# Attention, gated product and squared-ReLU layers on one core: the order of ScalarE and VectorE in attention written out by hand, and the first w3·w_out products in float32

## The chip, the cores and the metric

The kernel runs on one core of a Trainium2 chip. The metric is the device time of one execution in microseconds (us). The program before has a median of 604.52 us over 3 runs (602.40 to 607.51); the one execution that the profiler recorded took 602.16 us, of which 600.4 us lie between the first and the last instruction (the span).

## The reference, cut to what matters

```
attn:   scores = q kᵀ / 8, causal mask, softmax over keys (sum + 1e-9), times v
        2 batches x 12 heads x 448 tokens x 64
moe:    h = ((x w1) * (x w2)) w3 ;  y = h w_out        768 -> 1024 -> 1024 -> 768
moe2:   r = max(y w_in, 0) ; out = (r * r) w_out2      768 -> 2048 -> 768
```

There are 896 tokens. The weights come as float64 (8 bytes), all the rest as float32.

## The kernel before, in words

The matrix W = w3·w_out does not depend on the tokens, so it is worked out once, on TensorE, in between the steps of attention; then h·w_out needs one product by W in place of two. W has 16 rows of w3 blocks (two groups g of 8, `w3` 0 to 15) by 2 column halves: 32 *units*, each made by `w_half` from one w3 block and four w_out blocks, in one PSUM bank (`acc`), which is then copied or added into `wraw`.

A product of two float32 matrices is made of three matmuls of type fp32r: each factor is split into a high part and the rest (hi·hi + hi·lo + lo·hi). A unit is thus 4 blocks x 3 = 12 matmuls of 128x128 by 384 columns. A weight block goes through these steps before it can be used:

- `load`: one DMA into a raw buffer (3 of them, `RAW`), on the SP queue,
- `to_f32`: float64 to float32, by a Prelu on ScalarE (ACT), a tensor_scalar on the low words on VectorE (DVE) and a shift-and-or (scalar_tensor_tensor) on DVE,
- `two_parts`: a cast to fp32r on ACT (the high part) and a subtraction on DVE (the low part).

Attention goes over 12 pairs of heads in 13 *slots*. In slot p TensorE (PE) has: the scores of pair p (`s`), a unit, the transposes of the probabilities of pair p-1 (`pp`, 20 of them, copied out of PSUM to `pt` by ACT), a unit, the product with v of pair p-1 (`x`), a unit. `fill` says where units are made: after each of three gaps of a slot, from gap `LEAD` on. For each head the softmax has four blocks of rows; each takes a fused minimum on DVE (custom instruction, from PSUM, into `p`), an exponential with a row sum on ACT, and, after two small operations on `st` on DVE, a division by the sum (tensor_scalar on `p`) on GpSimd (POOL), or on DVE for pair 0. The `x` product is split into two fp32r parts in `xT` by ACT and DVE.

PSUM has 2 banks (`ps_w`) that `acc` of the units and `x` share in turn, and 6 banks (`ps_a`) that the score tiles (6 for a pair) and the `pp` tiles (6 for a pair) share in turn. So a unit waits until what was in its bank two turns ago has been copied out, and transposes wait until the minima have read the scores.

The order of PE's instructions in attention is as the code writes it (`manual_schedule` with PE). On DVE, ACT, POOL and the SP queue a scheduler at build time sets the order, from priorities (`high_priority`, `AHEAD`, `FAR_AHEAD`, `issue_after`) and its own estimate of time. On the chip every engine runs its instructions strictly in that order; an instruction that waits holds up all behind it.

After attention TensorE goes through x·w1, x·w2, h = ab·W, g = h·w_in and g·w_out2, with weights converted in the same way into a ring of 8 buffers.

Of the kernel before, what the change touches and what calls it, by code (L numbers as in the profile page):

```python
# [17 lines left out]
def attention_moe_moe2(ctx: ExitStack, tc: tile.TileContext, qk, v, w1, w2, w3, w_out, w_in2, w_out2, out):  # L18
# [11 lines left out]

    nc = tc.nc
    NP_ALL, P, S2 = qk.shape
    S = S2 // 2
# [14 lines left out]
    RING = 8  # L48
    RAW = 3
    LEAD = 7  # L50
    EARLY = 2
    AHEAD, FAR_AHEAD = 120, 400

# [20 lines left out]
    def to_f32(key):  # L74
        t = raws.pop(key)
        n = t.shape[1]
        low, high = t[:, :, 0], t[:, :, 1]
        x = rawp.tile([P, DM], F32, tag="x", name=f"x_{key[0]}_{key[1]}", bufs=2)[:, :n]
        nc.scalar.activation(x, high.bitcast(F32), AF.Prelu, scale=2.0 ** -112, alpha=-2.0 ** 32)  # L79
        nc.vector.tensor_scalar(low, low, 2.0 ** -29, 7.0, ALU.mult, ALU.min)  # L80
        nc.vector.scalar_tensor_tensor(  # L81
            x.bitcast(U32), x.bitcast(U32), 3, low, op0=ALU.logical_shift_left, op1=ALU.bitwise_or)
        f32s[key] = x
# [16 lines left out]
    for g in range(N3 // KF):  # L100
        for i in range(KF):
            order += [("w3", g * KF + i)]
            if g == 0 and i == 0:
                order += [("wout", f) for f in range(NB)]
            if g == 0 and i % 2 == 1:
                order += [("wout", NB + i // 2)]
# [13 lines left out]
    def make_f32(n):  # L120
        for key in order[made["f32"]:n]:
            make_loads(made["f32"] + 1)
            if key[0] != "W":
                to_f32(key)
            made["f32"] += 1

    def make(key):

        while made["hl"] <= place[key]:
            i = made["hl"]  # L130
            nm, n = at = order[i]
            make_f32(i + 2)
            make_loads(i + 2 + RAW)
            if nm == "w3":
                t = w3p[0].tile([P, 2, W3N], F32R, tag="w3", name=f"w3_{n}", bufs=2)
            else:
                t = ringp.tile([P, 2, DM], F32R, tag="ring", name=f"hl_{nm}_{n}")
            two_parts(t[:, 0], t[:, 1], wraw[:, n, :] if nm == "W" else f32s.pop(at))
            hls[at] = t
# [11 lines left out]
    with (  # L151
# [14 lines left out]
        st_t, p_t, pt_t = {}, {}, {}  # L166
# [14 lines left out]
        def scores(p):  # L181

# [12 lines left out]
            for g in BLOCKS:  # L195
                for i in g:
                    w = (i + 1) * CP
                    for j in range(2):
                        own = slice(j * D, (j + 1) * D)
                        mm(ps[j, i], y[own, 0, i * CP:w], y[own, 1, :w], True, True)  # L200
            for j in range(2):
                for g in BLOCKS:
                    for i in g:
                        last["min"] = nc.vector.tensor_tensor_reduce(  # L204
                            p_t[2 * p + j][:, off[i]:off[i + 1]], ps[j, i], mask[:, S - (i + 1) * CP:], QS, 3.0e38,
                            ALU.add, ALU.min, st_t[p][:, 0, j, i:i + 1],
                        ).ins

        def softmax(p, j):

            st = st_t[p][:, :, j]
            blocks = [(i, p_t[2 * p + j][:, off[i]:off[i + 1]]) for g in BLOCKS for i in g]
            for i, e in blocks:
                nc.scalar.activation(e, e, AF.Exp, bias=st[:, 0, i:i + 1], scale=-1.0,  # L214
                                     accum_out=st[:, 1, i:i + 1])
            nc.vector.tensor_scalar(st[:, 2], st[:, 1], 1.0e-9, None, ALU.add)
            nc.vector.reciprocal(st[:, 3], st[:, 2])
            engine = nc.vector if p < 1 else nc.gpsimd
            for i, e in blocks:
                engine.tensor_scalar(e, e, st[:, 3, i:i + 1], None, ALU.mult)  # L220
# [3 lines left out]
        def p_transposes(h):  # L224
            pt = p_t.pop(h)
            t = att.tile([CP, off[NCH]], F32, tag="pt", name=f"pt{h}", bufs=3)
            for gi, g in enumerate(((0,), (1,), (2, 3))):
# [8 lines left out]
                last["pt"] = nc.scalar.copy(t[:, coff[g[0]]:coff[g[0]] + o], x[:CP, :o]).ins  # L236
            pt_t[h] = t

        def attend(p):
# [3 lines left out]
            for c in range(NCH):  # L243
                for j in range(2):
# [3 lines left out]
                       c == 0, c == NCH - 1)  # L248
            b, kk = p // NPAIR, p % NPAIR
            hi, lo = (xT[:, s, kk, b * S:(b + 1) * S] for s in range(2))  # L250
            two_parts(hi, lo, x)
# [3 lines left out]
        last = {}  # L255

        def w_half(g, i, n):
# [3 lines left out]
            for f in range(NB):  # L261
                with tc.high_priority(AHEAD):
                    make(("wout", g * NB + f))
                    make(("w3", min(n3 + 1, N3 - 1)))
                t, c = hls["w3", n3], slice(f * P, (f + 1) * P)
                wo = hls["wout", g * NB + f]
# [227 lines left out]
```

## Time and profile before

| | |
|---|---|
| median of 3 runs | 604.52 us (602.40 to 607.51) |
| profiled execution | 602.16 us, span 600.4 us |
| PE busy | 573.8 us (96%) |
| DVE busy | 282.8 us (47%) |
| ACT busy | 275.3 us (46%) |
| POOL busy | 163.9 us (27%) |
| mean granted TensorE clock | 0.98 |

Attention and the units end at 184.7 us; from there on TensorE alone works through the dense layers. The page cuts the span in 40 slices of 15 us: PE's first slices are the ones below nine tenths, and in the second and third the granted clock (tenths of full speed) is 6 and 7. Busy shares are averages over stages that have different limits, so they are read stage by stage. A duration of one instruction includes its latency; instructions that follow each other at once overlap by some tens of ns, so that a start-to-start distance is a little shorter.

### The profile page before, as it was taken

The page shows a single profiled execution, that of the slowest core. Times are in us where ns is not written, and L with a number is a line of the kernel's source. Part 1 is how long each engine was busy: PE and PEld are TensorE (multiplying, and loading weights), DVE is VectorE, ACT ScalarE, POOL GpSimd, SP SyncE. Part 2 cuts the span into 40 slices and gives each one's busy share as a digit, 9 for nine tenths or more (in the row PEclk, how much of TensorE's full clock was granted, in tenths as well). Part 3 has the DMA queues.
Part 4 walks back from the last instruction along what each step waited for, and adds up shares of the span by engine and source line. Part 5 has one row for each costly group of instructions (what it writes and reads, how often), then busy time and mean ns, then how long its engine had stood idle before and what let it go on. Part 6 is the DMA issues. An engine that isn't in the chain of part 4 may idle for free.

```text
span 600.4 us, 8072 instructions
## 1 busy us (share of the span) xinstructions
PE 573.8 (96%) x3120; PEld 511.3 (85%) x3120; DVE 282.8 (47%) x557; ACT 275.3 (46%) x584; POOL 163.9 (27%) x144
## 2 busy tenths in 40 slices
PE   5769898999989999999999999999999999999997
PEld 3458676888779999999999999999999999999997
DVE  4877576676766555411120177555300875421111
ACT  5877776676765433222210166555301755551000
POOL 1285677557650211111110001333100013331000
PEclk9679999999989999999999999999999999999999
DMA  8664334432345343300000056333300663000111
GB/s 300 239 217 150 133 117 153 123 106 91 130 160 219 139 159 105 106 1 1 0 1 1 0 198 222 106 105 106 106 0 1 208 224 118 29 2 27 52 53 52
DMA packets 14821, 63.95 MB, mean 107 GB/s; under 512 B 1664, under 2 KB 1920, under 8 KB 14784
## 3 DMA queue, kind: packets, MB, share of 16 engines
q1 hardware_dynamic: 14784, 63.45, 31.2%
q8 instruction: 24, 0.39, 0.3%
q14 instruction: 13, 0.11, 0.1%
HBM read 60.69 MB, written 2.75 MB: 106 GB/s over the span
## 4 chain that ended last, share of the span: by engine, by line
PE 78%; DVE 8%; DMA 7%; ACT 4%; issue 1%; SPq 0%; DVEq 0%
PE w L63 25%; PE g L63 20%; PE o L63 19%; PE h L63 10%; DMA raw_w<-in_w 7%; DVE p L204 2%; PE x L63 2%; PE pp L232 2%; DVE x_w L81 1%; ACT p L214 1%; ACT pt L236 1%; PE s L63 1%; DVE raw_w L80 1%; DVE x_wout L81 1%; DMA raw_wout<-in_w_out 1%
## 5 line engine op out<-in xcount | busy, mean ns | idle before, releaser
L220 POOL TENSOR_SCALAR p<-p,st 112x448 f32<-112x448 f32 (+1 forms) x88 | 99.9, 1152 | 72.9 <-ACT p L214 24.7
L63 PE MATMUL w<-xT,hl_w 128*128 128x448 f32 x576 | 119.5, 368 | 0.0
L63 PE MATMUL g<-hT,hl_win 128*128 128x448 f32 x576 | 119.4, 368 | 0.0
L63 PEld LDWEIGHTS w<-xT,hl_w 128*128 128x128 f32 x576 | 108.0, 188 | 11.0
L63 PEld LDWEIGHTS g<-hT,hl_win 128*128 128x128 f32 x576 | 108.1, 188 | 10.9
L63 PE MATMUL o<-hl_wout,gT 128*128 128x384 f32 x672 | 116.8, 334 | 0.0
L63 PEld LDWEIGHTS o<-hl_wout,gT 128*128 128x128 f32 x672 | 116.5, 188 | 0.1
L87 POOL TENSOR_TENSOR gT<-r,gT 128x448 fp32r<-128x448 f32 x32 | 40.1, 1275 | 198.1 <-ACT gT L86 130.1
L63 PE MATMUL w<-hl_wout,w 128*128 128x384 f32 x384 | 77.6, 351 | 5.0 <-ACT wraw L275 2.6
L63 PEld LDWEIGHTS w<-hl_wout,w 128*128 128x128 f32 x384 | 67.8, 194 | 9.6 <-ACT wraw L275 3.0
L214 ACT ACTIVATE p<-p,st 112x112 f32<-112x112 f32 (+2 forms) x96 | 50.2, 536 | 21.4 <-DVE st L204 21.4
L63 PE MATMUL h<-abT,hl_W 128*128 128x448 f32 x288 | 59.7, 368 | 0.0
L63 PEld LDWEIGHTS h<-abT,hl_W 128*128 128x128 f32 x288 | 54.1, 188 | 5.5
L87 POOL TENSOR_TENSOR abT<-a,abT 128x448 fp32r<-128x448 f32 x16 | 22.3, 1408 | 108.4 <-ACT abT L86 108.4
L87 DVE TENSOR_TENSOR hl_wout<-x_wout,hl_wout 128x768 fp32r<-128x768 f32 x24 | 23.5, 981 | 40.0 <-ACT hl_wout L86 39.9
L204 DVE CUSTOM_DVE_ANT_0 p<-s,mask 112x112 f32<-112x112 f32 (+2 forms) x96 | 37.8, 443 | 8.7 <-PE s L63 8.5
L232 PE MATMUL pp<-ident,p 112*112 112x112 f32 x240 | 30.5, 279 | 11.4 <-POOL p L220 5.9
L232 PEld LDWEIGHTS pp<-ident,p 112*112 112x112 f32 x240 | 26.0, 143 | 15.7 <-POOL p L220 6.9
L63 PE MATMUL s<-qk 64*112 64x112 f32 (+3 forms) x192 | 30.5, 448 | 6.6 <-DMA qk<-in_qk 4.0
L81 DVE SCALAR_TENSOR_TENSOR x_wout<-x_wout,raw_wout 128x768 uint32<-128x768 uint32 x24 | 33.4, 1391 | 5.9 <-ACT x_wout L79 5.9
L414 ACT ACTIVATE r<-g 128x448 f32<-128x448 f32 x32 | 15.8, 542 | 43.7 <-PE g L63 43.7
L79 ACT ACTIVATE x_w<-raw_w 128x512 f32<-128x512 f32 (+1 forms) x32 | 25.5, 800 | 21.0 <-DVE hl_w L87 8.7
(49 smaller groups left out, 491.2 us busy)
## 6 DMA issues: line engine op xcount, KB each, us to landing
raw_wout<-in_w_out SPq DMA_DIRECT2D x24, 768.0 KB, 4.5
raw_w<-in_w SPq DMA_DIRECT2D x16, 768.0 KB, 4.4
raw_win<-in_w_in SPq DMA_DIRECT2D x16, 768.0 KB, 4.3
raw_w<-in_w SPq DMA_DIRECT2D x16, 512.0 KB, 3.7
qk<-in_qk SPq DMA_DIRECT2D x12, 448.0 KB, 4.3
v<-in_v SPq DMA_DIRECT2D x12, 224.0 KB, 3.2
out<-acc SPq DMA_DIRECT2D x6, 384.0 KB, 2.3
out<-acc SPq DMA_DIRECT2D x2, 192.0 KB, 1.9
```

Source lines behind the costliest of these rows:

```text
L63: return nc.tensor.matmul(o, l, r, start=start, stop=stop)
L79: nc.scalar.activation(x, high.bitcast(F32), AF.Prelu, scale=2.0 ** -112, alpha=-2.0 ** 32)
L80: nc.vector.tensor_scalar(low, low, 2.0 ** -29, 7.0, ALU.mult, ALU.min)
L81: nc.vector.scalar_tensor_tensor(x.bitcast(U32), x.bitcast(U32), 3, low, op0=ALU.logical_shift_left, op1=ALU.bitwise_or)
L87: (engine or nc.vector).tensor_tensor(lo, x, hi.bitcast(F32), op=ALU.subtract)
L204: last["min"] = nc.vector.tensor_tensor_reduce(p_t[2 * p + j][:, off[i]:off[i + 1]], ps[j, i], mask[:, S - (i + 1) * CP:], QS, 3.0e38, ALU ...
L214: nc.scalar.activation(e, e, AF.Exp, bias=st[:, 0, i:i + 1], scale=-1.0, accum_out=st[:, 1, i:i + 1])
L220: engine.tensor_scalar(e, e, st[:, 3, i:i + 1], None, ALU.mult)
L232: nc.tensor.transpose(x[:CP, o:o + CP], pt[:, off[i] + c * CP:off[i] + (c + 1) * CP], ident[:CP, :CP],)
L236: last["pt"] = nc.scalar.copy(t[:, coff[g[0]]:coff[g[0]] + o], x[:CP, :o]).ins
L414: nc.scalar.activation(r, o[b], AF.Relu)
```

## The change

On ACT and DVE, too, the order in attention becomes the one in the code (`manual_schedule` with PE, DVE and Activation; all priorities go). POOL and SP stay with the scheduler.

- The minima (`minima`), exponentials (`exps`), sums and divisions (`divide`) of a head and the split of `x` (`x_parts`) are functions of their own, called at fixed places of a slot. All eight minima of a pair now stand together, head 0 first.
- Conversions are made in a `step`: at a set place it takes one block `a` from raw to float32 and splits one block `b` in two parts, the instructions of the two interleaved. There is one step in slot 0, 5 in slot 1 (none of which splits), 4 in slot 2 and 3 in each later slot.
- The units of the first two w3 blocks (`PLAIN = 2`: 4 units) multiply float32 by float32, 4 matmuls in place of 12, straight from the float32 blocks (`xw`, and a `w3` buffer). These two w3 blocks are never split; the first four w_out blocks are split later, in slot 2, for the units from the third w3 block on.
- The division of the second head is on DVE for pairs 0, 1 and 2 (before: both heads of pair 0); the first head of pair 0 goes to POOL.
- `LEAD` is 5 for 7: units begin one gap earlier, and one gap of slot 7 gets none. `wraw` of the first group is copied by DVE for both halves (before: the first half by ACT).
- The loads of v and of q, k are asked for one slot later; w_out blocks 4 to 7 come in the places of w3 blocks 3 to 6.

```diff
+    def convert(a=None, b=None):
+        if b:
...
+            x = wraw[:, n, :] if nm == "W" else f32s[b] if whole(b) else f32s.pop(b)
+            nc.scalar.copy(t[:, 0], x)
...
+            nc.scalar.activation(y, high.bitcast(F32), AF.Prelu, scale=2.0 ** -112, alpha=-2.0 ** 32)
+            nc.vector.tensor_scalar(low, low, 2.0 ** -29, 7.0, ALU.mult, ALU.min)
...
+        if b:
+            nc.vector.tensor_tensor(t[:, 1], x, t[:, 0].bitcast(F32), op=ALU.subtract)
+        if a:
+            nc.vector.scalar_tensor_tensor(
+                y.bitcast(U32), y.bitcast(U32), 3, low, op0=ALU.logical_shift_left, op1=ALU.bitwise_or)
...
-            engine = nc.vector if p < 1 else nc.gpsimd
+            engine = nc.vector if p < NEAR and j == 1 else nc.gpsimd
...
+                if n3 < PLAIN:
+                    mm(acc, f32s["w3", n3][:, c], f32s["wout", f][:, cols], f == 0, f == NB - 1)
+                    continue
...
-        with tc.manual_schedule(engines={mybir.EngineType.PE}):
+        with tc.manual_schedule(engines={ET.PE, ET.DVE, ET.Activation}):
...
+                    scores(p)
+                    if p > 2:
+                        step()
+                    minima(p)
+                    exps(p, 0)
...
+                fill()
+                if softmax:
+                    divide(p, 0)
+                if attn_v:
+                    p_transposes(2 * (p - 1))
+                    p_transposes(2 * (p - 1) + 1)
+                    for _ in range({1: NB - 1, 2: 2}.get(p, 1)):
+                        step(split=p > 1)
+                if softmax:
+                    exps(p, 1)
+                fill()
+                if attn_v:
+                    attend(p - 1)
+                    if softmax:
+                        divide(p, 1)
+                    x_parts(p - 1)
+                    for _ in range({2: 2}.get(p, 1)):
+                        step(split=p > 1)
+                fill()
```

What this does to the order, at the three places that matter below. First DVE, from the first instruction of attention on: the minima of pair 0 (ISA; the rows of size 112x1 read the minimum out) and the first w3 block (`raw_w_0`). Before:

```order
L204 ISA p_0_100,st_99<-s_0_3_101,mask 112x448
L204 ISA st_99 112x1
L204 ISA p_1_104,st_99<-s_1_3_105,mask 112x448
L204 ISA st_99 112x1
L204 ISA p_0_100,st_99<-s_0_2_102,mask 112x336
L204 ISA st_99 112x1
L80 TENSOR_SCALAR raw_w_0_326<-raw_w_0_326 128x512
L204 ISA p_1_104,st_99<-s_1_2_106,mask 112x336
```

With the change, the same place, the last rows of the minima of pair 0 and what follows:

```order
L233 ISA p_1_110,st_105<-s_1_0_113,mask 112x224
L233 ISA st_105 112x1
L98 TENSOR_SCALAR raw_w_0_97<-raw_w_0_97 128x512
L103 SCALAR_TENSOR_TENSOR w_0_134<-w_0_134,raw_w_0_97 128x512
L246 TENSOR_SCALAR st_105<-st_105 112x4
L247 RECIPROCAL st_105<-st_105 112x4
L233 ISA p_0_155,st_154<-s_0_3_156,mask 112x448
```

The first instruction that needs a weight moved from behind three minima to behind eight, and it now stands ahead of all minima of pair 1.

Second PE, behind the scores of pair 2 (`s_1_0_250`; a unit has the name `w_0` or `w_1` by its column half). Before:

```order
L63 MATMUL s_1_0_250<-qk_136 112x224
L232 MATMUL pp_0_282<-ident,p_0_149 112x112 x4
L232 MATMUL pp_1_288<-ident,p_0_149 112x112 x3
L232 MATMUL pp_2_293<-ident,p_0_149 112x112 x3
L232 MATMUL pp_0_299<-ident,p_1_153 112x112 x4
L232 MATMUL pp_1_305<-ident,p_1_153 112x112 x3
L232 MATMUL pp_2_310<-ident,p_1_153 112x112 x3
L63 MATMUL w_0_325<-hl_wout_353,w_0_344 128x384 x3
L63 MATMUL w_0_325<-hl_wout_362,w_0_344 128x384 x3
```

With the change:

```order
L65 MATMUL s_1_0_292<-qk_152 112x224
L65 MATMUL w_0_313<-xw_189,w_0_134 128x384
L65 MATMUL w_0_313<-xw_235,w_0_134 128x384
L65 MATMUL w_0_313<-xw_241,w_0_134 128x384
L65 MATMUL w_0_313<-xw_247,w_0_134 128x384
L262 MATMUL pp_0_326<-ident,p_0_155 112x112 x4
L262 MATMUL pp_1_332<-ident,p_0_155 112x112 x3
```

The first unit moved ahead of the transposes of pair 1, and each of its blocks is one matmul instead of three.

Third DVE again, around the copy that frees the bank of a unit (`wraw`), in slot 2. Before, the copy of the second unit:

```order
L80 TENSOR_SCALAR raw_w_5_483<-raw_w_5_483 128x512
L87 TENSOR_TENSOR xT<-x_405,xT 128x448
L277 COPY wraw<-w_1_416 128x384
L87 TENSOR_TENSOR w_2_485<-x_w_2_470,w_2_485 128x512
L204 ISA p_0_431,st_430<-s_0_3_432,mask 112x448
```

With the change, the copies of the first (`w_0_313`) and the second unit (`w_1_381`):

```order
L307 COPY wraw<-w_0_313 128x384
L246 TENSOR_SCALAR st_284<-st_284 112x4
L247 RECIPROCAL st_284<-st_284 112x4
L98 TENSOR_SCALAR raw_w_2_245<-raw_w_2_245 128x512
L101 TENSOR_TENSOR hl_wout_359<-xw_189,hl_wout_359 128x768
L103 SCALAR_TENSOR_TENSOR x_w_2_361<-x_w_2_361,raw_w_2_245 128x512
L98 TENSOR_SCALAR raw_w_3_251<-raw_w_3_251 128x512
L101 TENSOR_TENSOR hl_wout_368<-xw_235,hl_wout_368 128x768
L103 SCALAR_TENSOR_TENSOR x_w_3_370<-x_w_3_370,raw_w_3_251 128x512
L307 COPY wraw<-w_1_381 128x384
```

Two conversion steps, each of which needs ACT's part first, now stand ahead of the copy of the second unit.

## Rows read from the trace of the kernel before

**Rows 1.** Windows: start:end, length, busy us of each engine, granted clock, DMA, GB/s.

```profile
4.00:52.55 48.55, 36.30 (x193) 25.13 (x194) 37.91 (x118) 35.12 (x91) 19.00 (x16) 0.79 0.69 239
52.55:109.55 57.00, 52.69 (x353) 42.21 (x353) 36.94 (x119) 42.27 (x118) 37.10 (x33) 1.00 0.41 137
109.55:184.71 75.16, 72.75 (x476) 59.36 (x475) 50.22 (x138) 51.51 (x136) 43.81 (x40) 0.98 0.41 134
184.71:600.40 415.69, 412.01 (x2102) 384.56 (x2101) 157.76 (x184) 145.09 (x240) 62.39 (x48) 1.00 0.24 81
```

**Rows 2.** Windows again, the stretch in which pair 0 goes through TensorE.

```profile
12.90:27.50 14.60, 9.71 (x45) 6.18 (x46) 13.80 (x46) 12.66 (x37) 0.58 (x1) 0.53 0.68 231
```

**Rows 3.** Timeline of PE: start us, duration us, line, tiles, [idle before <- releaser].

```profile
21.67 2.12 PE L232 MATMUL pp<-ident,p 112*112 112x112 f32 x10 [0.31 <-ACT pt L236]
...
35.85 0.43 PE L232 MATMUL pp<-ident,p 112*112 112x112 f32 x1 [3.93 <-POOL p L220]
...
50.47 2.08 PE L232 MATMUL pp<-ident,p 112*112 112x112 f32 x20
...
59.35 2.15 PE L63 MATMUL s<-qk 64*112 64x448 f32 x16
...
75.09 2.15 PE L63 MATMUL s<-qk 64*112 64x448 f32 x16
...
103.18 2.15 PE L63 MATMUL s<-qk 64*112 64x448 f32 x16
...
107.47 2.08 PE L232 MATMUL pp<-ident,p 112*112 112x112 f32 x20
109.33 2.34 PE L63 MATMUL w<-hl_wout,w 128*128 128x384 f32 x12
111.60 2.11 PE L63 MATMUL x<-pt,v 112*64 112x448 f32 x16
...
115.94 2.15 PE L63 MATMUL s<-qk 64*112 64x448 f32 x16
...
170.58 3.73 PE L63 MATMUL w<-hl_wout,w 128*128 128x384 f32 x12 [2.40 <-DVE xT L87]
...
182.46 2.25 PE L63 MATMUL w<-hl_wout,w 128*128 128x384 f32 x12
```

**Rows 4.** Timeline of DVE, first 21 us.

```profile
5.99 0.62 DVE L204 CUSTOM_DVE_ANT_0 p<-s,mask 112x448 f32<-112x448 f32 x1 [5.99 <-PE s L63]
...
10.52 0.43 DVE L80 TENSOR_SCALAR raw_w<-raw_w 128x512 uint32<-128x512 uint32 x1 [2.93 <-DMA raw_w<-in_w]
...
16.61 0.96 DVE L81 SCALAR_TENSOR_TENSOR x_wout<-x_wout,raw_wout 128x768 uint32<-128x768 uint32 x1
...
17.57 1.16 DVE L220 TENSOR_SCALAR p<-p,st 112x448 f32<-112x448 f32 x4
18.65 0.95 DVE L87 TENSOR_TENSOR hl_wout<-x_wout,hl_wout 128x768 fp32r<-128x768 f32 x1
```

**Rows 5.** DVE groups by form: busy us, mean ns of one.

```profile
L87 DVE TENSOR_TENSOR w<-x_w,w 128x512 fp32r<-128x512 f32 x16 | 11.9, 744 | 0.5 <-ACT w L86 0.2
...
L81 DVE SCALAR_TENSOR_TENSOR x_w<-x_w,raw_w 128x512 uint32<-128x512 uint32 x16 | 11.1, 701 | 2.4 <-ACT x_w L79 2.4
...
L277 DVE COPY wraw<-w 128x384 f32<-128x384 f32 x8 | 4.4, 548 | 0.5 <-PE w L63 0.5
```

**Rows 6.** The page's costliest groups: minima (DVE) and exponentials (ACT).

```profile
L214 ACT ACTIVATE p<-p,st 112x112 f32<-112x112 f32 (+2 forms) x96 | 50.2, 536 | 21.4 <-DVE st L204 21.4
...
L204 DVE CUSTOM_DVE_ANT_0 p<-s,mask 112x112 f32<-112x112 f32 (+2 forms) x96 | 37.8, 443 | 8.7 <-PE s L63 8.5
```

**Rows 7.** Timeline of ACT: a pair's six copies of transposes, one Prelu.

```profile
53.37 2.30 ACT L236 COPY pt<-pp 112x448 f32<-112x448 f32 x6
...
68.75 0.91 ACT L79 ACTIVATE x_wout<-raw_wout 128x768 f32<-128x768 f32 x1
```

**Rows 8.** Timeline of POOL: the first three heads that it divides.

```profile
26.92 15.13 POOL L220 TENSOR_SCALAR p<-p,st 112x448 f32<-112x448 f32 x12 [24.73 <-ACT p L214]
```

More of the change, by code (lines that the diff above doesn't have):

```diff
@@ L104, in attention_moe_moe2 @@
                 order += [("wout", f) for f in range(NB)]
[L105 to L106 removed]
+            if g == 0 and NB - 1 <= i < 2 * NB - 1:
+                order += [("wout", i + 1)]
     order += ring[KF:]
@@ L130, in make @@
             i = made["hl"]
-            nm, n = at = order[i]
+            at = order[i]
             make_f32(i + 2)
             make_loads(i + 2 + RAW)
[L134 to L139, printed above, removed]
+            convert(b=at)
             made["hl"] += 1
@@ L235, in p_transposes @@
                         o += CP
-                last["pt"] = nc.scalar.copy(t[:, coff[g[0]]:coff[g[0]] + o], x[:CP, :o]).ins
+                nc.scalar.copy(t[:, coff[g[0]]:coff[g[0]] + o], x[:CP, :o])
             pt_t[h] = t
@@ L269, in w_half, with free, step @@
                        f == 0 and (s, r) == (0, 0), f == NB - 1 and (s, r) == (1, 0))
-            with tc.high_priority(FAR_AHEAD):
-                dst = wraw[:, i, cols]
-                if g > 0:
-                    nc.vector.tensor_tensor(dst, acc, dst, op=ALU.add)
-                elif n == 0:
-                    nc.scalar.copy(dst, acc)
-                else:
-                    nc.vector.tensor_copy(dst, acc)
+            dst = wraw[:, i, cols]
+            if g > 0:
+                nc.vector.tensor_tensor(dst, acc, dst, op=ALU.add)
+            else:
+                nc.vector.tensor_copy(dst, acc)
         units = [(g, i, n) for g in range(N3 // KF) for i in range(KF) for n in range(2)]
         NU = len(units)
+        parts = [key for key in order if not (key[0] == "w3" and key[1] < PLAIN)]
+        steps = [0, 0]
+        def free(key):
+            if key[0] == "w3":
+                return done[1] >= 2 * (key[1] - 1)
+            k = in_ring.get(key, 0) - RING
+            return k < 0 or k < NB and done[1] >= NU // 2
+        def step(f32=True, split=True):
+            a, b = order[steps[0]], parts[steps[1]]
+            spare = sum(not whole(k) for k in f32s) < XB
+            b = b if split and b in f32s and free(b) else None
+            a = a if f32 and a[0] != "W" and spare else None
+            convert(a, b)
+            steps[0] += a is not None
+            make_loads(steps[0] + RAW)
+            steps[1] += b is not None
         SLOTS = NP_ALL + 1
@@ L323, in attention_moe_moe2 @@
                 fill()
-        assert not units
-        make(ring[KF + 2])
-        with tc.issue_after(last["min"]):
-            make(ring[RING + NB - 1])
+        assert not units and all(k in hls for k in ring[:KF])
+        made.update(f32=steps[0], hl=steps[1] + PLAIN)
         for f in range(KF):
```

127 lines of the change are left out of this document (69 added, 58 removed).

## The prediction, made before the result was known

> **What bounds the kernel now.** I read the windows by stage first, to see in which stage TensorE (PE) stands still. From 184.71 us on PE is busy 412.01 of 415.69 us at full clock [rows 1]; the rest is the end of the kernel, and the change does not touch that stage. All that can be won lies ahead of 184.71. There the first stage, to the end of the transposes of pair 2 at 50.47 + 2.08 = 52.55, is the bad one: PE busy 36.30 of 48.55 us at a clock of 0.79, while VectorE (DVE) is busy 37.91 [rows 1, 3]. From there to the end of the transposes of pair 6 (109.55) PE has 52.69 of 57.00 us, and to the end of attention 72.75 of 75.16, clock 0.98 [rows 1].
>
> The timeline of PE gives the price of a slot without waits: from the scores at 103.18 to those at 115.94, 12.76 us. Of it a unit takes 111.60 - 109.33 = 2.27, the transposes 109.33 - 107.47 = 1.86 [rows 3]. The timeline of DVE shows why the start is bad: after three minima DVE meets an instruction that needs the first weight, and stands for 2.93 us with the other minima behind it [rows 4]. Later PE waits 3.93 us for a head that POOL divides [rows 3]. From 12.90 to 27.50 the granted clock is 0.53, so mostly the lower level, 1.2 GHz, after PE had little to do [rows 2].
>
> **Stage 1, to the end of the transposes of pair 2.** I lay the new order out with durations of the rows, whole durations, so that hand-overs between engines are covered.
>
> - The eight minima of pair 0 begin at 5.99 [rows 4] and take 8 x 0.443 = 3.5 us [rows 6]: 9.5. The first w3 block: its tensor_scalar 0.43 [rows 4] and 0.70 [rows 5]: 10.7. With 0.3 for the two small sums (my estimate), POOL starts head 0 of pair 0 at 11.0. Three heads took it 15.13 us [rows 8], one 5.04: 16.1. DVE does the other head in 1.16 [rows 4] meanwhile.
> - PE has been idle since about 11, so I take 1.2 GHz, at which ten transposes took 2.12 [rows 2, 3]: 20 of them end at 20.3, ACT's last copy (a sixth of 2.30, [rows 7]) at 20.7.
> - ACT then makes the Prelu of three w_out blocks, 3 x 0.91 [rows 7], and the exponentials of the second head of pair 1, 4 x 0.536 [rows 6]: 25.6.
> - DVE: sums 0.3, division 1.16, split of x 0.6 (taken as the copy from PSUM, [rows 5]), the second w3 block 0.70: 28.4. Then the minima of pair 2 can run. DVE did little but wait for ACT from 17 to 25; I name this because it is what would be late next.
> - ACT's exponentials of pair 2 end near 31.2, its six copies at 33.5. Behind them stand the two steps of the third order excerpt: cast 0.9 (taken as the Prelu), then on DVE 0.95, 0.70, 0.43, 0.95, 0.70 [rows 4, 5]: 38.15, and the copy of the second unit 0.55: 38.7. Only then has the third unit a bank; PE, ready near 37, waits 1.7 us.
> - From 38.7: DVE divides and splits x, w_out 2 and 3 (2 x 0.95), copies (0.55), splits w3 2 (0.74): 44.1. The minima of pair 3 free the banks for the transposes of pair 2: these end at 47.5.
>
> Before, that point was 52.55, with 3 units done; now it is 47.5 with 4. Gain 5.05 + 2.27 = **7.3 us**.
>
> The float32 units are inside this. The trace of before has no float32 matmul of this shape. Its nearest row is the product with v: 16 records of float32 for 2 x 1120 columns in about 2.0 us [rows 3]. If the two heads, which use different halves of the array, run side by side, a block of 384 columns costs 384/1120 x 2.0 = 0.7 us and a unit 2.8; if they do not, 1.4. I take 2.8, because the 16 records there are twice the 8 matmuls of the program, which looks like several passes; the lower end stays in the range. Two of the four units lie under DVE's chain, two on the path, so the ends are 2 x (1.4 - 2.8) = -2.8 and 0. The Trainium skill (FP8 and Floating Point Precision, TensorE Precision Notes) has a rule that speaks against this edit: true FP32 takes 4 passes through the array, one more than three fp32r products. By that rule a unit would cost 4/3 of 2.27, 3.0 us, and the sum would be 0.4 us longer; no run here shows that shape yet. As work for DVE the edit saves little: two splits of 0.74 go, eight copies of 0.55 come from ACT, and one division of 1.16, so that DVE has some 4 us more in attention. What it does is let units start before the splits.
>
> **Stage 2, transposes of pair 2 to pair 6.** Slots 3 to 5 carry three full steps each. From the end of the transposes, T: ACT first made the next exponentials (they end 0.5 before T), then its copies to T + 1.8, cast 0.6, Prelu 0.91: 3.3; DVE 0.96 and the copy of the unit 0.55: 4.8, where PE wants the bank at 2.27 + 2.0 = 4.3; exponentials to 5.4, sums and x to 6.4, step to 8.6, copy 9.1, step (0.5 + 0.74 + 0.96) 11.4, minima 2.9 (they overlap by the 0.08 of their reads): 14.3, last transposes 14.6. So about 14.4, 14.6 and 14.2 for three slots and 12.9 for the lighter slot 6: 56.1 against 57.0. Gain **0.9 us**. These slots stay bound by DVE and ACT; bounds are 12.76 (PE alone) and 75.09 - 59.35 = 15.74, the longest slot of before [rows 3].
>
> **Stage 3, to the end of attention.** Before lost here a wait of 2.40 us for the split of x, and the unit behind it took 3.73 instead of 2.34 at a lowered clock: 3.8 us [rows 3]. In the new order the split of x stands right behind the division, no conversion of a w1 block ahead of it, and the steps are light, so I take this away but leave 0.8 for transposes that wait for POOL in the last slot. Gain **3.0 us**; bounds 0 and 4.5.
>
> **Sum.** 7.3 + 0.9 + 3.0 = 11.2 us off the profiled execution's 602.16: 591. That execution is the fastest of those shown, 0.4% under their median of 604.52; half of that offset put on, I predict **592 us** as a median. From no change this measurement can tell about 1%: under 598.5 is faster, over 610.6 slower.
>
> **Rivals.**
>
> *The clock eats it* (chance 0.20). The plan holds a PE wait of about 1.7 us near 38. In before the wait of 2.40 was followed by the lower clock and a unit of 3.73 [rows 3]. If that happens here the unit and scores up to the transposes run at half speed, about 4.8 us, and if the late wait of stage 3 comes back in another place, 3.0 more: 600. For it: the first stage of before lost half of its clock this way [rows 2]. Against it: the stretch 52.55 to 109.55 kept 1.00 with PE busy 52.69 of 57.00 [rows 1].
>
> *DVE in one line becomes the bound of all slots, slower* (0.10). A unit's bank is free only when DVE gets to its copy, and that copy now always stands behind a step that waits for ACT; before, ACT made half of the copies of the first group. If every slot from 3 to 11 takes the 15.74 us of before's longest, 9 x 2.98 = 26.8 us are lost where my plan has 6.9: 612. It decides when the copy comes later than 4.3 us after the transposes; the plan has 4.8 in three slots, and light steps after that. Against it: DVE's own work is about 12.3 us of a full slot and far less from slot 6 on.
>
> *Better than planned* (0.10). The first transposes run at 2.4 GHz (-2.3) and full slots at PE's 12.76 (-5.1): 585.
>
> The forecast has 0.56; 0.04 is for what I did not think of, a late DMA above all: raw buffers are freed three steps, some 10 us, before they are needed, so I cost the moved loads of v, q and k and the SP queue at nothing, and a late one would cost what the first weight did, 2.93.
>
> **Range.** The forecast's own range is 585 to 598 (full slots between -5 and +3.5, units -2.8, stage 3 between -1.5 and +3). With the first rival taken in: 584 to 604. Faster 0.70 (forecast, the better case, a part of the first rival), within 1% 0.20, slower 0.10.
>
> **What would show it.** DVE runs eight minima from 6 us without the wait of 2.93; the transposes of pair 2 end near 47.5 and those of pair 6 near 103.6 with 16 units done; three slots of about 14.5, then 12.8; no wait of 2.4 near the end; the last unit over at least 11 us earlier than 184.7 (matmuls of x·w1 that stood ahead of it now stand behind); float32 units of 2.8. I am wrong if pair 2's transposes end after 50, if slots 7 to 11 stay above 13.5, or if the stage after attention changes by more than 1 us.

## The result, and the profile after

The changed kernel takes **587.37 us** (median of 4 runs, 586.89 to 587.60) against 603.46 (4 runs, 601.95 to 607.51) for the kernel before beside it: ratio 0.9712, 95% interval 0.9678 to 0.9745. Predicted were 592 us, with a range of 584 to 604. The profiled execution took 587.25 us, its span is 585.4 in place of 600.4: 15.0 us shorter.

The windows by stage, cut at the same events as in [rows 1] (end of the transposes of pair 2, of pair 6, end of the last unit, to 0.04 us); the columns are start:end, length, busy time of PE, PEld, DVE, ACT and POOL, granted clock, DMA share, GB/s:

```profile
4.10:47.57 43.47, 35.88 (x189) 21.94 (x190) 35.20 (x118) 31.40 (x87) 16.77 (x13) 0.92 0.73 248
47.57:100.97 53.40, 52.69 (x354) 41.08 (x353) 42.77 (x127) 41.35 (x114) 39.29 (x33) 1.00 0.52 171
100.97:167.64 66.67, 66.21 (x454) 54.34 (x454) 43.85 (x131) 46.81 (x130) 44.07 (x40) 1.00 0.34 107
167.64:585.40 417.76, 414.12 (x2113) 386.52 (x2111) 161.40 (x192) 149.00 (x244) 61.13 (x48) 1.00 0.26 87
```

The first stage ends 4.98 us earlier, with four units done in place of three: with 2.27 for that unit a gain of 7.25. The second is 53.40 in place of 57.00, gain 3.60. The third of before, 75.16, less the ten matmuls of x·w1 that stood ahead of its last unit (182.46 - 180.29 = 2.17) and less the unit that is now done in stage 1 (2.27), is 70.72; now it is 66.67, gain 4.05. The rest of the kernel is 417.76 against 415.69 + 2.17 = 417.86. The sum is 15.0, the whole difference. The row of those ten matmuls, and the two longest waits of before in the second stage, both for a copy of `wraw` that ACT made (the change has DVE make it):

```profile
72.79 2.37 PE L63 MATMUL w<-hl_wout,w 128*128 128x384 f32 x12 [1.40 <-ACT wraw L275]
...
100.88 2.37 PE L63 MATMUL w<-hl_wout,w 128*128 128x384 f32 x12 [1.19 <-ACT wraw L275]
...
180.29 2.32 PE L63 MATMUL w<-xT,hl_w 128*128 128x448 f32 x10
```

The timeline of PE (start, duration, line, tiles, idle time before and what ended it), with the rows that answer [rows 3]:

```profile
14.81 0.43 PE L262 MATMUL pp<-ident,p 112*112 112x112 f32 x1 [3.83 <-DVE st L247]
15.71 3.79 PE L262 MATMUL pp<-ident,p 112*112 112x112 f32 x19 [0.46 <-POOL p L250]
...
24.47 2.85 PE L65 MATMUL w<-xw,w 128*128 128x384 f32 x8
28.98 2.82 PE L262 MATMUL pp<-ident,p 112*112 112x112 f32 x20 [1.66 <-DVE st L233]
...
37.95 2.85 PE L65 MATMUL w<-xw,w 128*128 128x384 f32 x8 [1.52 <-DVE wraw L307]
40.73 2.15 PE L65 MATMUL s<-qk 64*112 64x448 f32 x16
...
45.49 2.08 PE L262 MATMUL pp<-ident,p 112*112 112x112 f32 x20
...
58.25 2.64 PE L262 MATMUL pp<-ident,p 112*112 112x112 f32 x20
...
71.93 2.82 PE L262 MATMUL pp<-ident,p 112*112 112x112 f32 x20
...
85.73 2.50 PE L262 MATMUL pp<-ident,p 112*112 112x112 f32 x20
...
160.17 1.07 PE L262 MATMUL pp<-ident,p 112*112 112x112 f32 x9 [0.46 <-POOL p L250]
```

The long stops of before (3.93 for POOL, 2.40 for the split of x) are gone. What is left: 3.83 ahead of the first transposes, 1.66 for the minima of pair 2, 1.52 for the copy of the second unit, transposes of pairs 3 to 5 that take 2.64, 2.82 and 2.50 us where those of pair 2 take 2.08, and 0.46 for POOL near the end.

The start of the timeline of DVE, against [rows 4]: the minima begin at 6.09 and the first weight's conversion comes at 10.01 behind all eight, without a wait. POOL's first head and the clock of the window of [rows 2] follow:

```profile
6.09 0.62 DVE L233 CUSTOM_DVE_ANT_0 p<-s,mask 112x448 f32<-112x448 f32 x1 [6.09 <-PE s L65]
...
10.01 0.42 DVE L98 TENSOR_SCALAR raw_w<-raw_w 128x512 uint32<-128x512 uint32 x1
...
14.82 1.45 DVE L250 TENSOR_SCALAR p<-p,st 112x448 f32<-112x448 f32 x4
```

```profile
11.71 3.93 POOL L250 TENSOR_SCALAR p<-p,st 112x448 f32<-112x448 f32 x4 [9.53 <-DVE st L247]
```

```profile
12.90:27.50 14.60, 12.04 (x60) 7.56 (x60) 11.69 (x34) 10.62 (x26) 8.92 (x8) 0.77 0.85 285
```

The granted clock there is 0.77 in place of 0.53.

### The profile page after: what moved, and what is told of

Its sections match the earlier page's. It is cut to its first block, busy times and chain, and to the rows that moved or that the text cites. A ratio compares the mean times of both kernels' runs of the same rounds, so it can differ in the third digit from the quotient of the medians.

```text
span 585.4 us, 8034 instructions
## 1 busy us (share of the span) xinstructions
PE 568.9 (97%) x3104; PEld 503.9 (86%) x3104; DVE 283.2 (48%) x567; ACT 269.8 (46%) x574; POOL 162.9 (28%) x140
## 4 chain that ended last, share of the span: by engine, by line
PE 87%; ACT 5%; DVE 4%; issue 2%; DMA 1%; POOL 1%; POOLq 0%; DVEq 0%; ACTq 0%
PE w L65 29%; PE g L65 20%; PE o L65 20%; PE h L65 10%; PE s L65 3%; PE pp L262 3%; PE x L65 2%; ACT p L240 2%; ACT pt L266 1%; DVE p L233 1%; POOL p L250 1%; DMA raw_wout<-in_w_out 1%; DMA qk<-in_qk 1%; DVE x_w L103 0%; DVE p L250 0%
## 5 line engine op out<-in xcount | busy, mean ns | idle before, releaser
L65 PE MATMUL w<-hl_wout,w 128*128 128x384 f32 x336 | 65.8, 344 | 0.4 <-DVE wraw L307 0.2
L65 PEld LDWEIGHTS w<-hl_wout,w 128*128 128x128 f32 x336 | 57.4, 188 | 4.3 <-DVE wraw L307 1.1
L240 ACT ACTIVATE p<-p,st 112x448 f32<-112x448 f32 (+1 forms) x96 | 49.8, 532 | 24.3 <-DVE st L233 24.1
L233 DVE CUSTOM_DVE_ANT_0 p<-s,mask 112x448 f32<-112x448 f32 (+1 forms) x96 | 36.5, 444 | 6.9 <-PE s L65 6.9
L101 DVE TENSOR_TENSOR hl_wout<-x_wout,hl_wout 128x768 fp32r<-128x768 f32 x20 | 19.1, 957 | 41.6 <-ACT hl_wout L85 41.5
L65 PE MATMUL s<-qk 64*112 64x112 f32 (+3 forms) x192 | 28.3, 431 | 4.2 <-DMA qk<-in_qk 4.1
L266 ACT COPY pt<-pp 112x336 f32<-112x336 f32 (+1 forms) x72 | 28.4, 481 | 7.5 <-PE pp L262 7.2
L103 DVE SCALAR_TENSOR_TENSOR x_w<-x_w,raw_w 128x768 uint32<-128x768 uint32 (+1 forms) x30 | 26.1, 874 | 10.9 <-ACT x_w L97 10.3
```

Source lines behind the costliest of these rows:

```text
L65: return nc.tensor.matmul(o, l, r, start=start, stop=stop)
L101: nc.vector.tensor_tensor(t[:, 1], x, t[:, 0].bitcast(F32), op=ALU.subtract)
L103: nc.vector.scalar_tensor_tensor(y.bitcast(U32), y.bitcast(U32), 3, low, op0=ALU.logical_shift_left, op1=ALU.bitwise_or)
L233: nc.vector.tensor_tensor_reduce(e, ps[j, i], mask[:, S - (i + 1) * CP:], QS, 3.0e38, ALU.add, ALU.min, st_t[p][:, 0, j, i:i + 1],)
L240: nc.scalar.activation(e, e, AF.Exp, bias=st_t[p][:, 0, j, i:i + 1], scale=-1.0, accum_out=st_t[p][:, 1, j, i:i + 1])
```

## The experiments

All twelve were timed beside the kernel before, whose median was 603.17, 602.87 and 603.83 us in the three sessions (603.46 with the change). The change itself was timed in a session of its own, so a difference of a few tenths against it proves little by itself. "T" is the end of the transposes of pair 2.

| run | T, us | units done by T | median, us (runs) |
|---|---|---|---|
| before | 52.55 | 3 | 603.46 |
| the change | 47.57 | 4 | 587.37 (586.89 to 587.60) |
| e1 weight ahead of minima | 48.58 | 4 | 588.28 (587.85 to 588.49) |
| e5 old order of loads | 48.20 | 4 | 587.83 (587.62 to 588.05) |
| e6 both | 51.46 | 4 | 590.87 (589.85 to 591.91) |
| e14 before, new load | 54.32 | 3 | 604.41 (602.50 to 607.30) |
| e2 all divisions on POOL | 48.81 | 4 | 588.15 (588.11 to 588.23) |
| e3 no float32 units, late start | 50.16 | 3 | 591.50 (591.37 to 592.03) |
| e9 float32 units, late start | 47.75 | 3 | 589.56 (589.01 to 589.89) |
| e4 before, with float32 units | 56.43 | 3 | 607.73 (607.01 to 613.49) |
| e7 step behind the minima | 47.61 | 4 | 584.99 (584.89 to 585.33) |
| e8 e7, slot 2 step later | 47.57 | 4 | 584.48 (584.05 to 584.87) |
| e12 e7, second block later | 46.69 | 4 | 583.94 (583.86 to 585.56) |
| e13 e12, slot 2 step later | 45.53 | 4 | **583.34** (583.10 to 583.88) |

### Is stage 1 one chain? e1, e5, e6, e14

The prediction adds stage 1 up as one chain from the minima of pair 0. The rival: its engines have work enough to catch up a late start. e1 puts the conversion of the first weight ahead of the minima, e5 puts the loads in the order of before, e6 does both.

```diff
-                    if p > 2:
+                    if p > 2 or p == 0:
                         step()
                     minima(p)
                     exps(p, 0)
-                    if p == 0:
-                        step()
```

```diff
             load_pair(1)
-            make_loads(2)
             load_v(0)
+            load_v(1)
+            load_pair(2)
             make_loads(RAW)
```

> The changed kernel, but in slot 0 the conversion of the first w3 block stands ahead of the eight minima of pair 0 on DVE, as the scheduler had it in the kernel before, instead of behind them. Theory (stage 1 is one chain from the first minima to the transposes of pair 2, so whatever delays its head delays the end): the minima wait for the weight's load, which before landed 2.9 us after DVE could have used it; POOL's first head starts 2 to 4 us later than 11.71, the transposes of pair 2 end 2 to 4 us after 47.57, and the time is 2 to 4 us over 587.4. Rival (stage 1 is bound by the sum of DVE's and ACT's work, and a late head is caught up behind it): POOL's first head is late as well, but the transposes of pair 2 end less than 1 us later and the time rises by less than 1 us.

> The changed kernel, but the first transfers are issued in the order of the kernel before: q and k of pairs 0 and 1, v of both, q and k of pair 2, and only then the first w3 block and two w_out blocks. The conversion of the first w3 block stays behind the minima of pair 0. Theory (with the minima ahead, the weight has until 10.0 us to land, so the order of loads hardly matters): it lands near 10.5 as in the kernel before, everything behind it moves by 0.5 to 1 us, time 587.9 to 588.4. Rival (the gain of stage 1 comes largely from loads that the change issues earlier): 2.5 us or more over the changed kernel, 590 or more.

> As the run with the old order of loads, and besides the conversion of the first w3 block stands ahead of the minima of pair 0, as in the run with the weight ahead. There the weight landed at 7.69 and the start and the end of stage 1 both moved by about 1 us, too small a step to tell much. Here it should land near 10.5. Theory (one chain): POOL's first head starts near 15.3, the transposes of pair 2 end near 51.4, that is 3.5 to 4.5 us after the changed kernel's 47.57, and the time is 591 to 592. Rival (work-bound, a late head is caught up): POOL's first head is as late, but the end of stage 1 moves by less than 2 us, time under 589.5.

e1 came out 0.9 us over the change, less than its theory said and inside the rival's bound of 1 us: the weight landed at 7.69, early enough to hold the minima up little. POOL's first head started at 12.51 instead of 11.71 and T came 1.0 later. I had mis-sized the wait, and so small a step cannot tell the two theories apart. e5 came out 0.46 over, at the lower edge of what its theory said. In e6 the weight landed at 10.38 and the whole chain moved with it; one row each from the timelines of DVE, POOL and PE of e6, the last the transposes of pair 2:

```profile
10.38 0.43 DVE L98 TENSOR_SCALAR raw_w<-raw_w 128x512 uint32<-128x512 uint32 x1 [10.38 <-DMA raw_w<-in_w]
```

```profile
15.24 3.86 POOL L250 TENSOR_SCALAR p<-p,st 112x448 f32<-112x448 f32 x4 [13.05 <-ACT p L240]
```

```profile
49.38 2.08 PE L262 MATMUL pp<-ident,p 112*112 112x112 f32 x20
```

POOL's first head starts 15.24 - 11.71 = 3.5 us later than in the change, T comes 51.46 - 47.57 = 3.9 later, the time is 3.5 higher, just under the 591 that was expected. The chain theory holds, the rival falls. The four cells also say what the two edits are worth: either alone takes nearly all of the wait away (0.5 and 0.9 left), without both 3.5 us are lost. That the loads of v move behind the weight, which the prediction had costed at nothing, is a second protection of the same place.

e14 gives the new place of that load to the kernel before:

```diff
                 load_pair(1)
+                make_loads(1)
                 load_v(0)
```

> The kernel before, but the transfer of the first w3 block is issued ahead of those of v, as in the changed kernel; ACT and DVE stay ordered by the scheduler. Theory (the wait of 2.93 us in the kernel before is one for that load, and stage 1 is one chain): the wait shrinks to under 0.5 us, the transposes of pair 2 end 2 to 3 us ahead of 52.55, time 600 to 601. Rival (in the old order POOL's heads and the clock take it back): under 1 us gained, 602 to 603.

Neither came true: 604.41 against 603.83, ratio 1.001 (0.998 to 1.004). The timeline of DVE shows why nothing was tested:

```profile
5.92 0.62 DVE L204 CUSTOM_DVE_ANT_0 p<-s,mask 112x448 f32<-112x448 f32 x1 [5.92 <-PE s L63]
9.19 0.43 DVE L80 TENSOR_SCALAR raw_w<-raw_w 128x512 uint32<-128x512 uint32 x1 [2.63 <-DMA raw_w<-in_w]
```

The scheduler now put the conversion behind the first minimum, where before three minima stood ahead of it [rows 4], so DVE waits 2.63 us for the earlier load as it did 2.93 for the later one. The load also gained less than in e1: issued at 1.64, it was waited for until 9.19, in e1 until 7.69 with the same issue time; in before until 10.52. Asking for the load earlier gave nothing here, where the order was not fixed as well.

### Division of the second heads: e2

```diff
-    NEAR = 3
+    NEAR = 0
```

> The changed kernel with all divisions on POOL (NEAR = 0 instead of 3). Theory (in the first three slots POOL's heads, 3.9 to 6.2 us each, are on the chain): two heads of pair 0 one after the other delay the first transposes of head 1 by about 4 us, some of which the later ACT work hides; transposes of pair 2 end 3 to 5 us after 47.57, time 590.5 to 592.5. Rival (DVE's own work is the limit of stage 1, so that the 3 x 1.16 us that it is spared pay for the wait): no change within 1 us.

T moves by 1.24 us, the time by 0.78: far less than the theory's 3 to 5 us, and just inside the rival's 1 us. POOL's row:

```profile
11.61 12.26 POOL L250 TENSOR_SCALAR p<-p,st 112x448 f32<-112x448 f32 x12 [9.42 <-DVE st L247]
```

Pair 0's second head starts its transposes at 19.26; in the change all of pair 0's were then nearly over (15.71 + 3.79 = 19.50). In e2 they end at 22.01, 2.5 us later. Half of this is caught up: the wait of 1.66 us that the change has ahead of the transposes of pair 1 is gone in e2. So a second head that is 2.5 us late costs about half of that at T. The divisions that DVE is spared may be part of what is caught up; e2 does not tell. Second heads on DVE are worth about 0.8 us against all heads on POOL. No run has the division as before (both heads of pair 0 on DVE) in the new order.

### The float32 units: e3, e9, e4

e3 keeps the order and makes all units of split blocks; e9 keeps the float32 units and starts units as late as before; e4 gives the float32 units to the kernel before and leaves its order to the scheduler.

```diff
-    PLAIN = 2
-    LEAD = 5
+    PLAIN = 0
+    LEAD = 7
...
-                        step(split=False)
+                        step()
...
-                        step(split=p > 1)
+                        step()
...
-                        step(split=p > 1)
+                        step()
```

> The changed kernel's order alone: no w3 block is used in float32 (PLAIN = 0), the splits of the first w3 block and of four w_out blocks are made in slot 1 and 2, and the units start two gaps later as in the kernel before (LEAD = 7). Theory (float32 units are what lets TensorE start units before the splits, worth one unit of 2.27 us more in stage 1 and two to three splits of 0.74 to 0.95 us on its chain): transposes of pair 2 end between 48 and 51 with three units done instead of four, time 590 to 594. Rival (the written-out order alone explains all of the 15 us): at most 1 us over 587.4.

```diff
-    LEAD = 5
+    LEAD = 7
```

> The changed kernel with its float32 units, but the units start two gaps later, as in the kernel before (LEAD = 7 instead of 5). The run without float32 units had that start too, and the four-conversion splits in slots 1 and 2, and took 591.5. Theory (what the float32 form gives is mostly the earlier start: three units instead of four ahead of the transposes of pair 2, one unit of 2.27 us): 588.5 to 590, the transposes of pair 2 end between 45.5 and 48 with three units done, or nearly as late as in the changed kernel if DVE sets them. Rival (the splits that the float32 form spares on DVE and ACT ahead of the first units are what counts): within 0.7 us of 587.4.

Both theories held: e3 is 4.1 us over the change, e9 2.2 (its units begin one gap later, not two). From PE's timelines, first e3, then e9, the wait ahead of the transposes of pair 1; between them e3's last split on DVE ahead of them:

```profile
33.67 3.59 PE L262 MATMUL pp<-ident,p 112*112 112x112 f32 x20 [9.99 <-DVE st L233]
```

```profile
31.43 0.95 DVE L101 TENSOR_TENSOR hl_wout<-xw,hl_wout 128x768 fp32r<-128x768 f32 x1
```

```profile
28.62 3.95 PE L262 MATMUL pp<-ident,p 112*112 112x112 f32 x20 [4.53 <-DVE st L233]
```

In e3 five splits (of the first w3 block and four w_out blocks) stand on ACT and DVE ahead of the minima of pair 2, so the transposes of pair 1 start 5 us later than in e9. The start one gap earlier thus gives 2.2 us, and splits that come later or not at all give 1.9. That the earlier start needs the float32 form is not shown: no run starts split units one gap earlier, and in e3 the last of those splits ends at 31.43 + 0.95 = 32.38, 1.3 us ahead of the transposes, with TensorE idle. What e3 has in common with the change is worth the rest: 603.2 - 591.5 = 11.7 us of 16.1. That is the order of ACT and DVE, and with it the new places of loads and divisions and the copies of `wraw` on DVE, of which e5 prices the first loads at about 0.5 us and e2 the divisions at about 0.8; the copies were not tried by themselves.

> The kernel before, with the scheduler's order, and only the first four units in float32 (PLAIN = 2); divisions on POOL. Theory (the gain comes from the order of ACT and DVE; in the old order the first weight still stands ahead of the minima and the units come as late as before): the time falls by 0 to 3 us against the kernel before, 600 to 603.5. Rival (the float32 units carry the gain): it falls by 8 us or more, to 595 or below.

e4 fell outside both: 4.6 us *slower* than the kernel before, ratio 1.009 (1.005 to 1.013). PE's timeline, to be held against the 3.93 of before [rows 3] and its first unit, and POOL's; first the row of before, then e4's PE and e4's POOL:

```profile
38.77 3.13 PE L63 MATMUL w<-hl_wout,w 128*128 128x384 f32 x12
```

```profile
38.55 0.43 PE L247 MATMUL pp<-ident,p 112*112 112x112 f32 x1 [5.91 <-POOL p L235]
...
41.10 3.75 PE L64 MATMUL w<-xw,w 128*128 128x384 f32 x8
```

```profile
27.00 4.52 POOL L235 TENSOR_SCALAR p<-p,st 112x448 f32<-112x448 f32 x4 [24.82 <-ACT p L229]
34.49 9.25 POOL L235 TENSOR_SCALAR p<-p,st 112x448 f32<-112x448 f32 x8 [2.97 <-DVE st L232]
```

POOL, which in before worked through three heads without a break [rows 8], now stands 2.97 us for a reciprocal of pair 1 that the scheduler put on DVE behind splits and a conversion. The first unit still comes behind the transposes of pair 1, 2.3 us later than before, and the float32 units are longer: their earlier readiness has no use where they stand. As the scheduler changed the order around them, e4 does not price the float32 units alone in the order of before.

### Slots 3 to 5: e7

In the change ACT and DVE hand over to each other in a loop. In e7 the step that stood ahead of the minima of the slot's pair stands behind them:

```diff
-                    if p > 2:
-                        step()
                     minima(p)
+                    if p > 2:
+                        step()
                     exps(p, 0)
```

> The changed kernel, but in slots 3 to 11 the step that stands ahead of the minima of the slot's pair stands behind them, still ahead of the exponentials. Theory (slots 3 to 5 are one loop of ACT and DVE: in the changed kernel ACT waits 1.6 us for the first minimum, which stands behind a step on DVE; that wait then goes): slots 3 to 5 fall from 13.32, 13.86 and 13.48 to TensorE's own 12.75 to 12.9, 1.8 to 2.4 us in all, time 585.0 to 585.6. Rival (these slots are bound by the sum of DVE's work, whatever its order): slots unchanged, time within 0.5 us of 587.4.

The theory held: 584.99 us, 2.4 less. The transposes of pairs 2 to 6 in e7 follow each other at TensorE's own pace:

```profile
45.53 2.08 PE L262 MATMUL pp<-ident,p 112*112 112x112 f32 x20
58.28 2.08 PE L262 MATMUL pp<-ident,p 112*112 112x112 f32 x20
71.04 2.08 PE L262 MATMUL pp<-ident,p 112*112 112x112 f32 x20
83.79 2.08 PE L262 MATMUL pp<-ident,p 112*112 112x112 f32 x20
96.54 2.08 PE L262 MATMUL pp<-ident,p 112*112 112x112 f32 x20
```

Steps of 12.75, 12.76, 12.75, 12.75 in place of 13.32, 13.86, 13.48, 12.74 (from end to end in the change). The slots were bound by the order, not by the amount of work. In ACT's timeline of the change the loss shows as this wait, gone in e7:

```profile
71.82 0.67 ACT L240 ACTIVATE p<-p,st 112x448 f32<-112x448 f32 x1 [1.59 <-DVE st L233]
```

### The waits left in stage 1: e8, e12, e13

e8 is e7 with one of slot 2's two steps moved behind the copy of the second unit; e12 is e7 with the conversion of the second w3 block behind the minima of pair 2; e13 is both.

```diff
-                    for _ in range({1: NB - 1, 2: 2}.get(p, 1)):
+                    for _ in range({1: NB - 1, 2: 1}.get(p, 1)):
...
-                    for _ in range({2: 2}.get(p, 1)):
+                    for _ in range({2: 3}.get(p, 1)):
```

> As the run with the step behind the minima, and in slot 2 one of the two steps that stand ahead of the copy of the second unit is moved behind it. Theory (the third unit waits 1.52 us for that copy, on the chain of stage 1): the wait goes, the transposes of pair 2 end 0.7 to 1.5 us earlier than in that run, and the time falls by as much. Rival (DVE's work in one line up to the minima of pair 3 is what ends stage 1, and moving a step only moves the wait): the wait of the third unit goes, the transposes of pair 2 wait instead, and time changes by less than 0.3 us.

```diff
-                    if p > 2:
-                        step()
+                    if p > 1:
+                        step(split=p > 2)
                     exps(p, 0)
...
-                    for _ in range({2: 2}.get(p, 1)):
+                    for _ in range({1: 0, 2: 2}.get(p, 1)):
```

> As the run with the step behind the minima (584.99), and the conversion of the second w3 block, which stood on DVE ahead of the minima of pair 2, stands behind them. Theory (the transposes of pair 1 wait 1.45 us for the first minimum of pair 2, which on DVE stands behind that conversion of 0.42 and 0.69 us; stage 1 is one chain): they start about 1 us earlier than 29.02, the transposes of pair 2 end 0.7 to 1.1 us earlier than 47.6, time 583.9 to 584.4. Rival (DVE's work in one line up to the minima of pair 3 sets the end of stage 1): less than 0.3 us.

> As the run with the second block behind the minima, and one of the two steps ahead of the copy of the second unit moved behind it. Tried without the first edit, the third unit's wait of 1.53 us went, but TensorE waited 2.52 instead of 1.45 us ahead of the transposes of pair 1, its granted clock was 0.75 in the 6.9 us behind that, and the end of stage 1 stayed. Theory (that was the clock): with the first edit the wait ahead of the transposes of pair 1 is under 1.5 us, the clock stays at 1.00, and the transposes of pair 2 end 0.7 to 1.5 us earlier than in the run it starts from, time 582.6 to 583.7. Rival (DVE's work in one line): the third unit's wait goes, but the time stays within 0.3 us of that run.

In e8 the wait of the third unit went, T stayed at 47.57, and the median fell by 0.5 us; neither expectation had it so. The profiled execution is the slowest of e8's four (584.87). In it TensorE reached the transposes of pair 1 at 26.74, in e7 at 27.57, after an `x` of pair 0 that took less (rows of e7, then e8), and waited there longer; then e8's window:

```profile
19.42 3.29 PE L65 MATMUL x<-pt,v 112*64 112x448 f32 x16
```

```profile
19.35 2.53 PE L65 MATMUL x<-pt,v 112*64 112x448 f32 x16
...
29.26 3.50 PE L262 MATMUL pp<-ident,p 112*112 112x112 f32 x20 [2.52 <-DVE st L233]
```

```profile
29.20:36.10 6.90, 6.80 (x30) 4.73 (x32) 5.00 (x21) 6.90 (x21) 3.63 (x3) 0.75 0.45 151
```

The granted clock of 0.75 is a mean: part of the window ran at the lower level, 1.2 GHz. In e7, behind a wait of 1.45 us, the same window has a clock of 1.00. From the start of these transposes to the `x` behind them e8 took 6.65 us, e7 5.34. These 1.3 us, with a start 0.24 later, come to about the 1.53 that the edit had won. But the long wait is not the removed one come back: it ends at 29.26, and the step that the edit moves stands behind the minima of pair 2, which DVE begins at 28.48; up to there e7 and e8 have the same order. What this execution shows is a gain hidden by a wait and a clock that the edit did not cause.

e12 shortens e7's wait of 1.45 us at its source: transposes at 27.91 behind a wait of 0.55, T 0.92 us earlier, 583.94 us, as its theory said. In e13 slot 2's step then pays: the wait ahead of the transposes of pair 1 is 1.30, the window 29.20 to 36.10 is at 1.00, the third unit starts at 35.33 without a wait in place of 37.07, T is 45.53:

```profile
27.95 2.82 PE L262 MATMUL pp<-ident,p 112*112 112x112 f32 x20 [1.30 <-DVE st L233]
```

```profile
29.20:36.10 6.90, 6.85 (x38) 3.91 (x38) 5.59 (x20) 6.90 (x22) 3.79 (x4) 1.00 0.53 166
```

So e13 came out as its theory said: with the clock at 1.00 the edit shows its gain at T. Of the 1.16 us there 0.6 stay in the median; the next slot gives 0.3 back (13.07 us in place of 12.75, with a wait of 0.24 for a copy). e13, at **583.34 us** (ratio to before 0.966, 0.961 to 0.970), beats both kernels; none of its runs overlaps those of the change.

## Why the prediction was right, and where it was not

**Stage 1, right.** Predicted gain 7.3, measured 7.25; third unit at 38.7, measured 37.95; its wait 1.7, measured 1.52. That a late head moves the end of the stage was shown by e6. That the sums agree so well is partly luck. Two links were off and cancelled: POOL's first head began at 11.71 instead of 11.0 but took 3.93 instead of 5.04; and ahead of the exponentials of pair 1 stood a DMA that I had not foreseen, the fourth w_out block, issued at 17.82 when its raw buffer came free, 4.2 us ahead of its use where I had counted on some 10. ACT's row:

```profile
22.01 0.93 ACT L97 ACTIVATE xw<-raw_wout 128x768 f32<-128x768 f32 x1 [0.42 <-DMA raw_wout<-in_w_out]
```

The last link cancelled too. From the third unit on the plan has DVE's divisions, splits and minima decide, 47.5 - 38.7 = 8.8 us. In the trace TensorE works without a break from there to T, through two float32 units, scores and transposes, 47.57 - 37.95 = 9.62 us, so the end was TensorE's own; the third unit came 0.75 early and made up for it.

**A float32 unit at 2.8, right.** From the third unit's start to the scores behind it 40.73 - 37.95 = 2.78. The Trainium skill (FP8 and Floating Point Precision, TensorE Precision Notes) counts 4 passes for true FP32, from which an estimate would be 4/3 of 2.27, 3.0 us; the trace is 0.2 under that, and the measurement decides.

**Divisions, right in direction.** e2 gives the second heads on DVE 0.8 us.

**Stage 2, mis-sized.** The step that failed is "14.4, 14.6 and 14.2 for three slots": measured 13.32, 13.86 and 13.48, with the lighter slot at 12.74 for 12.9. That these slots are bound by the hand-overs of DVE and ACT was right, as e7 shows. But I chained whole durations. Rows of the change, three of ACT and three of DVE, each one behind the other:

```profile
60.02 2.29 ACT L266 COPY pt<-pp 112x448 f32<-112x448 f32 x6
...
62.18 0.87 ACT L85 CAST hl_wout<-x_wout 128x768 fp32r<-128x768 f32 x1
62.91 0.72 ACT L97 ACTIVATE x_w<-raw_w 128x512 f32<-128x512 f32 x1
```

```profile
69.68 0.96 DVE L101 TENSOR_TENSOR hl_wout<-x_wout,hl_wout 128x768 fp32r<-128x768 f32 x1
70.56 0.68 DVE L103 SCALAR_TENSOR_TENSOR x_w<-x_w,raw_w 128x512 uint32<-128x512 uint32 x1
71.16 0.62 DVE L233 CUSTOM_DVE_ANT_0 p<-s,mask 112x448 f32<-112x448 f32 x1
```

From start to start those of DVE take 0.88 and 0.60, 0.08 less than their durations; on ACT the next begins 0.13 and 0.14 ahead of the end. The Trainium skill (Perfetto Trace Analysis, DVE / Act Engine Instruction) lets a reported duration run to the acknowledged write, while the next instruction may begin to fetch before that; the rows agree, with 0.08 and 0.13 us. With two such hand-overs on ACT and some seven on DVE, up to the first minimum, that is an estimated 0.8 us a slot, 2.4 for three; 43.2 - 40.66 = 2.5 were missing. Two more terms were off in the slot of these rows and cancelled: ACT's copies end 1.42 us behind the transposes (60.89) where I had 1.8, and from the first minimum to the end of the next transposes it takes 3.59 where I had 3.2. The minima of this slot start 10.27 us behind the end of the transposes, where I had 11.4.

**Stage 3, a little small.** The wait of 2.40 and the slow unit behind it went, as predicted, and the wait for POOL in the last slot is 0.46 where 0.8 were left for it. Before also had transposes of 2.47 us at 158.49 and an `x` of 2.91 at 162.99, where 2.08 and 2.11 are usual; the granted clock there was 1.00, and the `x` had waits for ACT's copies within it. These went too, which I had not counted; the gain is 4.05 for 3.0, inside its bounds.

**After attention, right.** 417.76 against 417.86.

**The rivals.** The clock did not eat the gain: the transposes of pair 0 ran low, as planned, and behind the wait of 1.52 the unit took 2.85 at full clock. DVE in one line was not the bound of all slots: later slots take 12.75. "Better than planned" came true by half, in the full slots, though not in the first transposes; hence 587.4 instead of 592: of these 4.6 us stage 2 is 2.7 and stage 3 1.0, and about 1 is the half of the offset that I put on, which the change does not have (587.25 profiled, 587.37 median). The rival of DVE in one line also has a slip: it takes off 6.9 us for what my plan already has over 12.76 a slot, but the plan's slots come to 56.1 - 4 x 12.76 = 5.1, so its 612 should be about 614.

## What to carry to other kernels

Where one engine's instruction waits for a transfer, look at its place in the order and at the transfer's place together: moving the transfer alone gave nothing where a scheduler moved the instruction too (e14), while with a written order either one took away 2.6 to 3.0 of 3.5 us (e1, e5). In a chain of short instructions, count start to start: 0.08 to 0.14 us at each hand-over came to an estimated 0.8 us a slot here. And place optional work behind the instruction that the other engine is waiting for: moving one step behind the minima was worth 2.4 us with no work removed.

## What the runs showed of the hardware

- POOL took 3.93 us for a head at 11.71 and 6.17 for one at 18.26. Beside the first, DVE ran minima, which read PSUM and one tile of SBUF, and the first of a division; beside the second it ran these, with two tiles of SBUF as input, and tensor_scalars. Rows of POOL and DVE in the change:

```profile
18.26 6.17 POOL L250 TENSOR_SCALAR p<-p,st 112x448 f32<-112x448 f32 x4 [2.61 <-ACT pt L266]
```

```profile
20.81 0.96 DVE L103 SCALAR_TENSOR_TENSOR xw<-xw,raw_wout 128x768 uint32<-128x768 uint32 x1 [2.27 <-ACT xw L97]
...
23.92 0.96 DVE L103 SCALAR_TENSOR_TENSOR xw<-xw,raw_wout 128x768 uint32<-128x768 uint32 x1
```

  The Trainium skill (SBUF — State Buffer, Who interferes with whom) says that a DVE instruction with two SBUF inputs and a GpSimd instruction that reads SBUF contend; the rows fit that, and no run here took it apart.
- A transfer of the same 512 KB, issued at 1.63 us (e1) or 3.05 (e6), was waited for until 7.69 or 10.38: 1.4 us later in the queue, 2.7 later at its user. Issued at 1.64 in e14, with another order of transfers behind it, it was waited for until 9.19, so the time of issue alone does not give the time of landing.
- Behind a wait of TensorE of 2.52 us (e8) the granted clock of the window that followed, 29.20 to 36.10, was 0.75; behind 1.45 (e7) and 1.30 (e13) it was 1.00.
